# Adding x off TensorE for more output blocks, with query sums and query turns moved, in a fused attention and highway kernel

## The chip, the core and the metric

The kernel runs on one core of a Trainium2 chip. The metric is the device time of one execution in microseconds, as the median of several runs. All times below are in microseconds (us) unless marked ns. PE is TensorE, DVE is VectorE, ACT is ScalarE, POOL is GpSimd, SP is SyncE, which here only issues DMAs.

## The reference

For 8 batches with 8 heads, 576 tokens and a head width of 64, linear attention comes first, then a highway layer over 4608 rows of 512 features:

```python
q_s = softmax(q, axis=-1)          # over the 64 features of a head
k_s = softmax(k, axis=2)           # over the 576 tokens
kv  = einsum('bhsd,bhse->bhde', k_s, v)
x   = einsum('bhsd,bhde->bhse', q_s, kv)   # then heads side by side: 4608 x 512
H   = maximum(x @ w_h, 0)
T   = 1 / (1 + exp(-(x @ w_t + b_t)))
out = T * H + (1 - T) * x
```

Inputs and output are fp32; the kernel computes matmuls in fp16 and leaves out the subtraction of the maxima, which cancels.

## The kernel before, in words

**Tiles.** The unit of the attention part is a batch b, that of the highway part a chunk c of 512 columns, which is the batch of that number. Token s of a batch is 9p + n, so a batch has nine groups n of 64 tokens; n = 0 to 7 make up the chunk, and the ninth tokens (n = 8) of all batches are kept in x9 and done at the end as chunks 8 and 9, with 256 columns each. x is held with features on partitions, in four blocks ob (or k_) of 128 features. Two batches make a pair g = c // 2 (0 to 3), for the output has 128 rows per token group of a pair.

**Attention of a batch b.** exp_half (L183, ACT) takes exp of q and of k, half of the heads at a time. q_sums (L234, DVE, two instructions of 1.35) and q_recip (L252, DVE) give the reciprocal row sums, and q_scale_p (L264, POOL, 1.90 and 2.33) scales the queries. These then must be turned, features to partitions: for b up to 5 by q_trans (L69, PE, in three parts, each copied out by DVE at L282), for b = 6 and 7 by q_turn (L291), two transposing DMAs on SP's queue. cast_v (L195, POOL, two instructions of 1.15) casts v. kv_half (psk, PE) multiplies exp(k) and v, kv_norm (L222 and L223, DVE) divides, and x_pair (px, PE) multiplies by the turned queries, in two halves, each cast into xT by ACT (L354). With left=True it does the ninth tokens too, first of all in the first half, and x9_copy (L315, DVE) stores them.

**Highway, by chunk c and block ob.** W_h has the identity subtracted and is halved, so that

- gate (pt, PE, then tanh on ACT at L383) gives t = tanh((x W_t + b)/2),
- carry (ph on PE, then dd on DVE at L401) gives dd = max(-x/2, (x W_h - x)/2) = (H - x)/2,
- blend (DVE, L409) gives g = (t + 1) dd = T (H - x), in fp16.

The output is g + x. It is turned back to rows by matmuls with the identity (turn_block, L424), 128x128 each: one matmul for g and, accumulated in the same bank, one for x, unless add_x (L416, POOL) has added x to g in SBUF before. Which blocks are added so is listed in `added` (L414): blocks 0 and 1, and for the last pair also 2. out_tile(g, n) turns the four blocks of one token group of a pair and copies the bank to SBUF, mostly on ACT (L458); four of them are stored by one DMA. For the last pair (spare=True) more banks are used and DVE takes part of the copies (L454, L456). tile9 (L470) and last9 (L488) do so for ninth tokens, all with x turned on PE.

**Banks.** gate and carry take their banks from a pool of four (ps_ht). A bank is given out in the order in which banks became free in the program, and the trace shows it: the matmuls of a gate start after the dd of two blocks earlier at the soonest, those of a carry after the blend of two blocks earlier. q_trans and the ninth tokens of x_pair share one bank (q1), psk and x_pair share another two (q2), and out_tile has one of its own (nat).

**Order.** Each engine works through its instructions in program order. From chunk 1 on, that order is a list written by hand: `at(p, ...)` puts a step at position p, and the list is run by rising p, in the order of the calls where p is equal. Chunk c has gate(c, ob) at 8c + 2 ob, carry one later and blend two later, so one unit of p is half a block. Batch b has its steps around p = 8(b - 1) (L541), with offsets by batch (L543 to L563). The change's parts are all offsets in this list, the two lists of added blocks, the engine of some additions, and the copy of last9.

Of the kernel before, what the change touches and what calls it, by code (L numbers as in the profile page):

```python
# [18 lines left out]
def kernel(  # L19
# [10 lines left out]
    nc = tc.nc  # L30
    B, H, S, D = q.shape
    P = 128
    PAD = 128
    N9 = S // 64
# [46 lines left out]
    x9 = consts.tile([P, 4, B, 64], FP16, name="x9")  # L81
    g9 = consts.tile([P, 4, B, 64], FP16, name="g9")
# [77 lines left out]
    def two_banks(name, dt=FP32):  # L160
        return ps_2.tile([P, 2, 2048 // (4 if dt is FP32 else 2)], dt, tag="q2", name=name)
# [202 lines left out]
    def views(c):  # L364
        if c >= B:
            h = slice(4 * (c - B), 4 * (c - B) + 4)
            return lambda k_: x9[:, k_, h], lambda k_: g9[:, k_, h]
        g, b2 = c // 2, c % 2
        if g not in gT:
            gT[g] = gp.tile([P, 4, NM, 2, 64], FP16, tag="g", name=f"g_{g}")  # L370
        return lambda k_: xT[g][:, k_, :, b2, :], lambda k_: gT[g][:, k_, :, b2, :]
# [39 lines left out]
        )  # L411


    added = lambda g: (0, 1) if g < 3 else (0, 1, 2)  # L414

    def add_x(c, ob):  # L416
        xv, gv = views(c)
        nc.gpsimd.tensor_add(gv(ob), gv(ob), xv(ob))  # L418


    o32 = {}
# [2 lines left out]
    def turn_block(t, k_, xs, us):  # L424
        dst = t[:, k_, :]
        if xs is not None:
            mm(dst, xs, ident, True, False)
        mm(dst, us, ident, xs is None, True)

    def flat(t):  # L430
        return t.rearrange("p k d -> p (k d)")
# [35 lines left out]
    def blk9(t, g, k_):  # L467
        return t[:, k_, 2 * g : 2 * g + 2].rearrange("p b d -> p (b d)")

    def tile9(g, nk):  # L470
        if g % 2 == 0:
            o32["9", g // 2] = og.tile([P, 4, 512], FP32, tag="o32", name=f"o9_{g}")
        ps, tag = ((ps_1, "q1"), (ps_nat, "nat"))[g % 2]
        t = ps.tile([P, 4, P], FP32, tag=tag, name=f"nat9_{g}")
        for k_ in range(nk):
            turn_block(t, k_, blk9(x9, g, k_), blk9(g9, g, k_))
        o = o32["9", g // 2][:, g % 2, 0 : nk * P]
        if g % 2:
            nc.vector.tensor_copy(o, flat(t)[:, 0 : nk * P])
        else:  # L480
            nc.scalar.copy(o, flat(t)[:, 0 : nk * P])
        if g % 2:
            nc.sync.dma_start(
                rows9[:, g - 1 : g + 1, 0 : nk * P],
                o32["9", g // 2][:, 0:2, 0 : nk * P],
            )

    def last9():  # L488
        o9 = o32["9", 1]
        t = ps_ht.tile([P, 4, P], FP32, tag="ht", name="nat9_l")  # L490
        for i in range(2):
            turn_block(t, i, blk9(x9, i + 2, 3), blk9(g9, i + 2, 3))
        nc.scalar.copy(o9[:, 0, 384:512], t[:, 0])
        nc.vector.tensor_copy(o9[:, 1, 384:512], t[:, 1])
        nc.sync.dma_start(rows9[:, 2:4, 384:512], o9[:, 0:2, 384:512])


# [2 lines left out]
    def at(p, *fs):  # L500
        events.setdefault(p, []).extend(fs)

    E = lambda f, *a: (lambda: f(*a))

    for c in range(1, B + 2):
        for ob in range(4):
            p = 8 * c + 2 * ob
# [6 lines left out]
    for g in range(B // 2):  # L514
        p = 16 * (g + 1)
        if g < B // 2 - 1:
            for i in range(8):
                at(p + 2 + 2 * i, E(out_tile, g, i))
        else:
            for i in range(8):  # L520
                at(p + 1 + i, E(out_tile, g, i, True))
    p = 8 * B + 8
    at(p + 3, E(tile9, 0, 4))
    at(p + 4, E(tile9, 1, 4))
    at(p + 8, E(tile9, 2, 3), E(tile9, 3, 3), E(last9))

    at(8, E(cast_v_head, 2, 0, nc.gpsimd), E(q_scale_p, 2, 0, 4), E(q_scale_p, 2, 4, 8))
# [3 lines left out]
    at(10, E(cast_v_head, 2, 1, nc.scalar), E(exp_half, 2, "k", 1))  # L531
    at(10.5, E(blend, 0, 3))
    at(12.5, E(add_x, 0, 0), E(add_x, 0, 1), E(add_x, 1, 0))
    at(14.5, E(add_x, 1, 1))
    for c in range(2, B):
        for ob in added(c // 2):
            at(8 * c + 2 * ob + 2.5, E(add_x, c, ob))
    at(11, E(cast_v_head, 2, 2, nc.gpsimd), E(cast_v_head, 2, 3, nc.scalar))
    at(11, E(q_scale_p, 2, 8, N9))
    for b in range(2, B):  # L540
        p = 8 * (b - 1)  # L541
        if b > 2:
            e0, e1, s0, s1, sc = {  # L543
                3: (-2.6, -1.6, -1.1, -0.1, 1),
                4: (-5.5, -4.5, -2.8, -1.5, -1.4),
                5: (-5, -4, -3.4, -2.7, -2.6),
                6: (-6, -5, -4.9, -3.9, -3.8),
                7: (-6, -5, -4.9, -3.9, -3.8),
            }.get(b, (-5, -4, -3.9, -2.9, -2.8))
            at(p + e0, E(exp_half, b, "q", 0))  # L550
            at(p + e1, E(exp_half, b, "q", 1))
            at(p + s0, E(q_sums, b, 0))
            at(p + s1, E(q_sums, b, 1), E(q_recip, b))
            at(p + sc, E(q_scale_p, b, 0, 4), E(q_scale_p, b, 4, N9))
            s = p + {3: 0, 4: 0}.get(b, -0.5)
            at(s, E(exp_half, b, "k", 0), E(cast_v, b, 0))
            at(s + 0.9, E(cast_v, b, 1))
            at(s + 1, E(exp_half, b, "k", 1))
        tr, kv, x = {
            2: ((5, 6, 7.1), (4, 6.2), (6.5, 7.2)),  # L560
            3: ((3.5, 4.9, 4.95), (4, 4), (5.9, 6.9)),
            4: ((2, 3, 4), (4.5, 4.5), (5.9, 6.9)),
        }.get(b, ((2, 3, 4), (4, 4), (5, 6)))  # L563
        if b in turned:
            at(p - 2.05, E(q_turn, b, 0, 4), E(q_turn, b, 4, N9))
        else:
            for i in range(3):
                home = (lambda: two_banks("pq_t", FP16)[:, 0]) if b < 4 and i == 2 else None
                at(p + tr[i], E(q_trans, b, i, home))
        at(p + kv[0], E(kv_half, b, 0))  # L570
        if b == 2:
            at(p + kv[0], E(kv_norm, b, 0, 1))
            at(p + kv[1], E(kv_half, b, 1), E(kv_norm, b, 1, 2))
        else:
            at(p + kv[1], E(kv_half, b, 1), E(kv_norm, b))
        homes = (nat_bank, single) if b == 2 else None
        at(p + x[0], E(x_pair, b, 0, "AA" if b == 2 else "A", b > 2, homes))
        at(p + x[1], E(x_pair, b, 1, "AV" if b == 2 else "A", b > 2, homes))
# [70 lines left out]
```

## Time and profile before

| | us |
|---|---|
| median of 6 runs (131.12 to 132.03) | 131.54 |
| the profiled execution | 132.03 |
| its span, first to last instruction | 130.3 |
| PE busy (1395 matmuls) | 112.7 |
| DVE busy | 97.1 |
| ACT busy | 92.2 |
| POOL busy | 70.3 |

The profile is of one execution: for every instruction its start and length, and for idle time the instruction whose completion ended it. In a line such as `67.14 1.01 ACT L354 CAST ... [0.32 <-PE px L64]` the first number is the start from the beginning of the span, the second the length, and the bracket says how long the engine had been idle and for whom it waited. On DVE and ACT an instruction's record overlaps the next one's by up to 0.1, so distances are best taken from start to start. The mean granted TensorE clock was 0.992 of full speed. The DMA engines were busy nearly all of the time up to 86 us, with the loads of q, k and v, and partly so after that. In the last part, from 113 us, the last pair's output and the ninth tokens' work are interleaved.

### The profile page before, as it was taken

How to read it: one execution, taken by the hardware profiler on the slowest of the kernel's cores; microseconds unless marked ns; L12 is line 12 of the kernel's file. 1: busy time of each engine (PE TensorE's matmuls, PEld its weight loads, DVE VectorE, ACT ScalarE, POOL GpSimd, SP SyncE). 2: the span in 40 equal slices, each digit the busy share in tenths (PEclk: the TensorE clock that was granted, in tenths of full speed). 3: DMA queues.
4: the chain of work that ended last, by engine and by line, in shares of the span. 5: the costliest groups of instructions: out<-in, count | busy, mean ns of one | idle time of the engine just before them, and what ended most of it. 6: DMA issues, size and time to landing. Idle time of an engine off the chain costs nothing.

```text
span 130.3 us, 3405 instructions
## 1 busy us (share of the span) xinstructions
PE 112.7 (87%) x1395; PEld 62.2 (48%) x1395; DVE 97.1 (75%) x179; ACT 92.2 (71%) x130; POOL 70.3 (54%) x64
## 2 busy tenths in 40 slices
PE   4978996886967899999799998997979999999930
PEld 1325442353424445455454654453535455688920
DVE  1387355899799999799789899759945566769950
ACT  3553049994998679679899987996985757565520
POOL 2003436691289999709974983992899504500000
PEclk9999999999999999999999999999999999999996
DMA  3999999999999999999999999999059007065873
GB/s 115 368 379 373 398 401 411 413 410 412 406 410 413 401 410 411 409 407 377 331 400 405 358 273 408 408 241 373 15 115 378 15 0 327 0 282 244 362 296 115
DMA packets 20584, 41.25 MB, mean 317 GB/s; under 512 B 5460, under 2 KB 5976, under 8 KB 19544
## 3 DMA queue, kind: packets, MB, share of 16 engines
q1 hardware_dynamic: 20568, 41.03, 84.7%
q8 instruction: 11, 0.18, 0.5%
q14 instruction: 5, 0.04, 0.1%
HBM read 30.41 MB, written 9.44 MB: 306 GB/s over the span
## 4 chain that ended last, share of the span: by engine, by line
PE 34%; DVE 21%; POOL 14%; DMA 11%; issue 7%; ACT 6%; SPq 3%; DVEq 0%; POOLq 0%; ACTq 0%
PE pt L64 12%; DMA q<-in_q_dram 11%; PE ph L64 11%; POOL eq L264 8%; PE nat L64 5%; DVE dd L401 5%; DVE g L409 4%; DVE r L234 4%; POOL g L418 4%; PE psk L64 2%; ACT eq L183 2%; SPq L96 2%; PE pq L69 2%; PE px L64 2%; POOL v L195 2%
## 5 line engine op out<-in xcount | busy, mean ns | idle before, releaser
L264 POOL TENSOR_TENSOR eq<-eq,r 128x1024 f16<-128x1024 f16 (+2 forms) x16 | 29.7, 1872 | 14.4 <-DVE r L252 13.9
L64 PE MATMUL pt<-xT,w16t 128*128 128x512 f16 x128 | 34.0, 379 | 2.0 <-DVE dd L401 1.2
L64 PE MATMUL ph<-xT,w16h 128*128 128x512 f16 x128 | 33.3, 380 | 1.5 <-ACT w16h L116 1.1
L383 ACT ACTIVATE pt<-pt,bt 128x512 f32<-128x512 f32 (+1 forms) x40 | 24.8, 623 | 11.1 <-PE pt L64 9.8
L401 DVE SCALAR_TENSOR_TENSOR dd<-xT,ph 128x512 f16<-128x512 f16 x32 | 21.7, 679 | 8.1 <-PE ph L64 8.1
L409 DVE SCALAR_TENSOR_TENSOR g<-pt,dd 128x512 f16<-128x512 f32 (+1 forms) x40 | 25.2, 633 | 3.0
L418 POOL TENSOR_TENSOR g<-g,xT 128x512 f16<-128x512 f16 x18 | 20.5, 1151 | 7.4 <-DVE g L409 7.4
L64 PEld LDWEIGHTS <-w16t 128*128 128x128 f16 x160 | 14.7, 98 | 17.8 <-issue 5.1
L183 ACT ACTIVATE eq<-q 128x1152 f16<-128x1152 f32 x16 | 18.2, 1177 | 4.7 <-DMA q<-in_q_dram 4.7
L183 ACT ACTIVATE ek<-k 128x1152 f16<-128x1152 f32 x16 | 18.6, 1175 | 1.8 <-DMA k<-in_k_dram 1.8
L234 DVE TENSOR_REDUCE r<-eq 128x18 f32<-128x1152 f16 x12 | 16.2, 1346 | 4.8 <-ACT eq L183 4.8
L64 PEld LDWEIGHTS <-w16h 128*128 128x128 f16 x160 | 13.6, 98 | 11.7 <-ACT w16h L116 2.9
L195 POOL CAST v<-v 128x1152 f16<-128x1152 f32 x12 | 13.5, 1146 | 10.3 <-DMA v<-in_v_dram 10.3
L64 PE MATMUL nat<-ident,g 128*128 128x128 f16 x142 | 17.8, 219 | 1.2 <-POOL g L418 0.8
L64 PEld LDWEIGHTS <-g 128*128 128x128 f16 x144 | 13.7, 98 | 7.8 <-POOL g L418 1.2
L458 ACT COPY o<-nat 128x512 f32<-128x512 f32 x26 | 15.6, 602 | 0.4 <-PE nat L64 0.3
L354 ACT CAST xT<-px 128x1024 f16<-128x1024 f32 x10 | 10.2, 1016 | 5.3 <-PE px L64 5.3
L64 PE MATMUL warm<-wide,ident 128*128 128x512 f16 x41 | 11.7, 430 | 1.8 <-DVE wide L153 1.8
L69 PE MATMUL pq<-ident,eq 128*128 128x128 f16 x104 | 8.5, 219 | 3.4 <-DVE r L258 1.2
L69 PEld LDWEIGHTS <-eq 128*128 128x128 f16 x108 | 6.8, 98 | 7.6 <-POOL eq L264 2.3
L282 DVE COPY qsT<-pq 128x1024 f16<-128x1024 f16 (+1 forms) x16 | 9.3, 586 | 1.2 <-PE pq L69 0.7
L357 ACT CAST xT<-px 128x512 f16<-128x512 f32 x8 | 4.3, 590 | 7.8 <-PE px L64 7.8
(56 smaller groups left out, 108.8 us busy)
## 6 DMA issues: line engine op xcount, KB each, us to landing
out_dram<-o SPq DMA_DIRECT2D x8, 1024.0 KB, 4.6
q<-in_q_dram SPq DMA_DIRECT2D x7, 1152.0 KB, 13.9
k<-in_k_dram SPq DMA_DIRECT2D x7, 1152.0 KB, 13.2
v<-in_v_dram SPq DMA_DIRECT2D x5, 1152.0 KB, 13.9
v<-in_v_dram SPq DMA_DIRECT2D x6, 576.0 KB, 11.6
q<-in_q_dram SPq DMA_DIRECT2D x2, 576.0 KB, 4.2
k<-in_k_dram SPq DMA_DIRECT2D x2, 576.0 KB, 7.3
w32t<-in_moe_w_t_dram SPq DMA_DIRECT2D x1, 1024.0 KB, 11.6
```

What stands on the lines that cost most here:

```text
L64: mm = lambda o, l, r, st, sp: nc.tensor.matmul(o, l, r, start=st, stop=sp, skip_group_check=True)
L69: nc.tensor.matmul(o, i, ident, is_transpose=True, start=True, stop=True, skip_group_check=True,)
L183: nc.scalar.activation(dst[b][:, :, 2 * a : 2 * a + 2, :], in32[which][b][:, 2 * a : 2 * a + 2].rearrange("p c n d -> p n c d"), AF.Exp,)
L195: (eng or nc.gpsimd).tensor_copy(o, i)
L234: nc.vector.reduce_sum(qsum[b][:, :, h], eq[b][:, :, h, :], axis=AX.X)
L264: nc.gpsimd.tensor_mul(e, e, r.broadcast_to(list(e.shape)))
L354: copy[how](dst, t2.rearrange("p c (n d) -> p c n d", d=64))
L383: nc.scalar.activation(ps, ps, AF.Tanh, bias=bt2[:, ob : ob + 1], scale=0.5)
L401: nc.vector.scalar_tensor_tensor(dd, xv(ob), -0.5, ps, op0=ALU.mult, op1=ALU.max)
L409: nc.vector.scalar_tensor_tensor(gv(ob), th, 1.0, dd, op0=ALU.add, op1=ALU.mult)
L418: nc.gpsimd.tensor_add(gv(ob), gv(ob), xv(ob))
L458: nc.scalar.copy(o, flat(t))
```

## The change

- A third block (2) of pairs 1 and 2, the second and third pair, the fourth block (3) of the last pair, all four blocks of chunk 8 and blocks 0 and 1 of chunk 9 get x added before they are turned; the x matmuls of these blocks are left out of out_tile and tile9.
- For odd chunks the last of these additions (block 2 of chunks 3 and 5, block 3 of chunk 7) is on DVE, the others are on POOL. In chunk 7 and the ninth tokens the additions stand nearer behind their blends.
- The tiles of the last pair stand one position later.
- last9 copies its two blocks with one ACT instruction, not one on ACT and one on DVE.
- Batches 6 and 7: both query sums, formerly around the norm of the batch before (one ahead of it, one behind), stand behind it, and q_scale_p follows later, its second part 0.6 behind its first. The turning DMAs stand one position later.
- Batch 3: the first part of q_trans stands behind the following gate and output tile. Batch 4: its three parts stand about one position later, the third behind kv_half, kv_norm and the first sum of batch 5.

```diff
-    added = lambda g: (0, 1) if g < 3 else (0, 1, 2)
+    added = lambda g: ((0, 1), (0, 1, 2), (0, 1, 2), (0, 1, 2, 3))[g]
+    added9 = lambda g: (0, 1, 2, 3) if g < 2 else (0, 1)
...
-        nc.gpsimd.tensor_add(gv(ob), gv(ob), xv(ob))
+        late = ob == (3 if c == B - 1 else 2) and c % 2 and c < B
+        eng = nc.vector if late else nc.gpsimd
+        eng.tensor_add(gv(ob), gv(ob), xv(ob))
...
-            turn_block(t, k_, blk9(x9, g, k_), blk9(g9, g, k_))
+            turn_block(t, k_, None if k_ in added9(g) else blk9(x9, g, k_), blk9(g9, g, k_))
...
-        nc.scalar.copy(o9[:, 0, 384:512], t[:, 0])
-        nc.vector.tensor_copy(o9[:, 1, 384:512], t[:, 1])
+        nc.scalar.copy(o9[:, 0:2, 384:512], t[:, 0:2])
...
-                at(p + 1 + i, E(out_tile, g, i, True))
+                at(p + 2 + i, E(out_tile, g, i, True))
...
-    for c in range(2, B):
-        for ob in added(c // 2):
-            at(8 * c + 2 * ob + 2.5, E(add_x, c, ob))
+    for c in range(2, B + 2):
+        for ob in added(c // 2) if c < B else added9(2 * (c - B)):
+            at(8 * c + 2 * ob + (2.5 if c < B - 1 else 2.02), E(add_x, c, ob))
...
-                6: (-6, -5, -4.9, -3.9, -3.8),
-                7: (-6, -5, -4.9, -3.9, -3.8),
+                6: (-6, -5, -3.95, -3.1, -3),
+                7: (-6, -5, -3.95, -3.1, -3),
...
-            at(p + sc, E(q_scale_p, b, 0, 4), E(q_scale_p, b, 4, N9))
+            at(p + sc, E(q_scale_p, b, 0, 4))
+            at(p + sc + (0.6 if b > 5 else 0), E(q_scale_p, b, 4, N9))
...
-            3: ((3.5, 4.9, 4.95), (4, 4), (5.9, 6.9)),
-            4: ((2, 3, 4), (4.5, 4.5), (5.9, 6.9)),
+            3: ((4, 4.9, 4.95), (4, 4), (5.9, 6.9)),
+            4: ((3, 4, 4.9), (4.5, 4.5), (5.9, 6.9)),
...
-            at(p - 2.05, E(q_turn, b, 0, 4), E(q_turn, b, 4, N9))
+            at(p - 1.05, E(q_turn, b, 0, 4), E(q_turn, b, 4, N9))
```

## The prediction

> **What bounds the kernel now.** I read the page first (busy shares, slices, groups), then the chain that ended last in order of time, then the timelines of PE, DVE, ACT and POOL from 46 us on, line by line, mapped to the ordered list of steps; then the waits, and the DMA issues of the transposes.
>
> The page gives PE 87% of the span, DVE 75%, ACT 71%, POOL 54%; no share decides alone. Of the groups, shapes kept apart (count | busy us, mean ns | idle before, who ended it), these are touched:
>
> ```profile
> L418 POOL TENSOR_TENSOR g<-g,xT 128x512 f16<-128x512 f16 x18 | 20.5, 1151 | 7.4 <-DVE g L409 7.4
> ...
> L234 DVE TENSOR_REDUCE r<-eq 128x18 f32<-128x1152 f16 x12 | 16.2, 1346 | 4.8 <-ACT eq L183 4.8
> ...
> L64 PE MATMUL nat<-ident,xT 128*128 128x128 f16 x56 | 9.7, 219 | 0.0
> ```
>
> The chain in order of time (start, length, what) shows PE bounding most of 63 to 74, then DVE, PE, ACT, DVE, POOL, and PE alone from 97 to 118:
>
> ```profile
> 58.82 4.20 POOL eq L264 x2
> 63.02 0.05 issue
> 63.06 0.62 PE pq L69 x8
> ...
> 87.40 1.35 DVE r L234
> 88.75 0.60 DVE g L409
> 89.35 0.10 DVE rz L222
> ...
> 93.60 2.33 POOL eq L264
> 95.93 1.12 POOL g L418
> 97.09 0.45 PE nat L64 x5
> ```
>
> PE's timeline, in brackets the idle time just before: the four waits that the moved steps touch are kv norms behind a sum (78.50, 89.95), a v cast (87.83) and an added x (97.09).
>
> ```profile
> 78.50 0.22 PE L64 MATMUL px_l<-qsT,kvn 64*64 64x64 f16 x2 [0.44 <-DVE kvn L223]
> ...
> 87.83 0.48 PE L64 MATMUL psk<-v,ek 64*64 64x65 f16 x36 [0.26 <-POOL v L195]
> ...
> 89.95 0.22 PE L64 MATMUL px_l<-qsD,kvn 64*64 64x64 f16 x2 [0.68 <-DVE kvn L223]
> ...
> 97.09 0.23 PE L64 MATMUL nat<-ident,g 128*128 128x128 f16 x1 [0.82 <-POOL g L418]
> ```
>
> **The change, part by part.** Below, D is the time after minus the time before of the same PE step.
>
> *Removed matmuls.* Eight in each of three pairs (24), eight in the first two ninth tiles and four in the other two (12). Six turn matmuls take 0.34 in the chain, so 0.057 each: 2.05 us of PE in all. It counts only where PE sets the pace.
>
> *Added x.* POOL gets nine adds: three of 128x512 at 1.15 (its own row) and six of 128x256, at 0.61 by the 128x256 row of its scaling. They fall in its idle time, except add_x(4,2), which takes the place of add_x(4,1) between batch 6's scaling and its v casts. DVE gets three adds of 128x512 fp16. No such row exists; 128x288 took 0.31 and 128x1024 0.69, the nearest, 128x576, 0.45: I take 0.42, with 0.31 and 0.69 as ends (work is added, so no gain). The Trainium skill speaks against this: "GPSIMD Engine Reference", section 1 (Specifications), says the two engines share SBUF interfaces and contend when a DVE instruction has two SBUF inputs, which add_x has; two of them run beside POOL's scaling. The trace has one such meeting, DVE's add of 128x288 beside POOL's subtraction, against the same add alone:
>
> ```profile
> 21.35 0.42 DVE L246 TENSOR_TENSOR t<-t 128x288 f16<-128x288 f16 x1
> ...
> 33.93 0.31 DVE L246 TENSOR_TENSOR t<-t 128x288 f16<-128x288 f16 x1
> ```
>
> POOL's subtraction went from 0.43 (20.42) to 0.70 (22.21). Read as blocking, the rule would make add_x(5,2) wait out up to a whole 2.33 scaling; the row says a third more: 0.55. I take 0.55; blocking would cost about 0.7 there, since the scaling running then has that long to go.
>
> *Batch 3's turn, later.* PE idles before its first transposes at 49.94 until POOL's scaling is done. With gate(2,2) and out_tile(0,1) first, the gate starts at 49.59 and kv_half(3) is done at 52.12 instead of about 52.50; then the copy, the norm (kvn 52.79 instead of 53.18) and the second and third transposes follow in turn, and carry(2,2) starts at 52.95 instead of 53.36. Recip(4) and POOL's scaling of 4 (58.82) go with it. D = -0.41.
>
> *Batch 4's turn, later.* The idle time before 63.06 is filled with carry(3,1) and gate(3,2). But kv_half(4,1) waits for POOL's second v cast anyway: it follows the scaling by 2.23 (65.18 before, 64.80 after), so psk is done at 65.33, not earlier than D says. What is new: the copy of the third transposes, before at 65.03, in DVE's idle time ahead of the norm, now stands behind q_sums(5,0), and x_pair(4,0) on PE needs it first of all (ninth token, and the bank). DVE: norm 65.36 to 65.99, sum 65.91 to 67.25 (1.26 apart from the next), copy to 67.45. x_pair(4,0) starts at 67.50 instead of 66.61: a new PE wait of about 1.2, D = +0.89. Queued behind it on PE is everything, on ACT the cast of its output. DVE's dd(3,2) and recip(5) still come 0.2 early.
>
> *add_x(3,2) on DVE.* It pushes DVE by 0.35 to 0.5 (start to start), but with PE late DVE has idle time before dd(4,0) (72.5 to 72.93): nothing. Without that cover it costs its 0.35 at the copy before q_trans(5,1), 74.44. D = +0.8 there, and +0.75 at kv_half(5) after two shorter tiles.
>
> *Late sums, batch 6.* Now the norm of 5 needs only psk: done 77.85, kvn 78.52, and x_pair(5,0) starts right behind carry(4,2) at 78.72: the 0.44 is gone, D = +0.22. Both sums follow (moved past blend(4,1) and the third copy, whose start they no longer hold), so recip(6) starts at 81.07 instead of 79.74: 0.75 of D and 0.58 of DVE idling for psk. On POOL the scaling is moved past add_x(4,1), which runs in idle time before it; the chain after it keeps its length: scaling 81.62 to 85.8 (4.19), add_x(4,2) 1.11, casts 2.25 to 89.1. So kv_half(6,1) starts at 89.15 instead of 87.83: the wait of 0.26 becomes about 1.5 in two pieces, D = +1.32. This is where most of the gain goes.
>
> *Late sums, batch 7.* With the norm ahead of the sums the 0.68 goes: x_pair(6,0) at 90.53, D = +0.58. DVE from the norm: before, norm to the end of blend(4,3) took 5.36 with one sum in it (77.82 to 83.18); with two sums and an add 5.36 + 1.26 + 0.5 = 7.1, so blend(5,3) ends at 96.8. PE banks go back by dd and blend, so gates (6,0) and (6,1) lose about 0.4 and 0.25 to DVE. out_tile(2,0) no longer waits: add_x(5,1) now runs ahead of scaling 7 (-0.82, with its queueing). Carry(6,1) starts at 97.24 instead of 97.38: D = -0.14. Scaling 7 ends at 97.6; the casts end at 99.8, against kv_half(7,1)'s 99.69: D = 0 at x_pair(7,0), 101.2.
>
> *Query turns by DMA, later in the list.* SP's queue has nothing between the old and the new place, so they move past no DMA; they go when their scaling is done. Batch 6's second half goes at 85.85 (before 84.51), batch 7's at 97.65 (95.96). The view of DMA issues has landings of 3.1, 3.4 and 6.0 us. With 3.4, batch 7's lands at 101.05, just ahead of x_pair(7,0); hidden, with 0.15 to spare.
>
> *PE alone, 102 to 113.* ACT sets gate(7,0), so five shorter tiles count: 5 x 0.057 = 0.28. D = -0.28 at carry(8,0).
>
> *The tail.* DVE works from 116.08 almost without a break, but idled 0.90 just before. New: add_x(7,3) (+0.36), on which out_tile(3,0) waits (PE: last block at 114.57); PE is then half a microsecond ahead as tiles have four matmuls, not five or eight; the first copy out of the two banks stays at about 116.1, but dd(8,1) is by then done. With tiles one step later, dd and blend of one block no longer follow each other, which saves the 0.10 to 0.17 between dependent instructions four times (0.5). The POOL adds of the ninth tokens (0.61 after each blend) end at 120.4, as tile9 reaches them. Blend(9,3) ends at 124.1 instead of 125.03. One ACT copy of 128x256 takes the place of ACT 0.27 then DVE 0.29: between the 128x128 row (0.27) and the 128x384 row (0.48), 0.37; but SP needs 0.4 for the DMA before it, so this saves 0.1. The stores of pair 3 follow their copies (the second at 120.7, before 121.1) and are not the last. The last DMA is issued at about 125.1 instead of 126.09.
>
> *The sum.* -0.41 + 1.30 - 0.67 + 1.10 - 0.74 - 0.72 + 0.14 - 0.28 - 0.68 = -0.96 (the D's in order: -0.41, +0.89, +0.22, +1.32, +0.58, -0.14, 0, -0.28, -0.96). Against the profiled execution (span 130.3, 132.03 in all, 0.49 above the median) that is 129.3 and 131.1; against the median 131.54, 130.6.
>
> **The rivals.** *(a) The tail keeps its bound.* DVE is full there and gets an add more; if the 0.90 comes back as a wait for add_x(7,3) and the two-bank copy, only D = -0.28 remains: 131.3. For: DVE's copy waited for ACT's at 116.08, and ACT's place is no earlier. Against: 0.5 of the saving is in DVE's own order.
> *(b) Slower: a late transpose.* Batch 6's first turn took 6.0 to land while loads filled the DMA engines (busy share 1.0 to 85). If the second half, issued 1.34 later, takes 6.0, it lands at 91.85 and x_pair(6,0) starts 1.37 after my 90.53: 132.0. It decides from 4.7 us on. Against: the loads drain by about 87, and the second half before was in use at 89.95, at most 5.4 after its issue.
> *(c) The new wait at x_pair(4,0) is short.* If the copy isn't behind the sum, D stays near 0 there, and all after runs about 0.9 earlier down to the tail: 129.7. Against: the list fixes DVE's order.
>
> **How the numbers follow.** Forecast 130.6 with 0.44; (a) 131.3, 0.24; (b) 132.0, 0.16; (c) 129.7, 0.16. About 0.3% (0.39 us, so 131.15 and 131.93) is what a measurement of this kernel can tell from no change. Faster: nearly all of the forecast, all of (c), a little of (a): 0.62. Same: most of (a), some of the forecast and of (b): 0.22. Slower: the rest of (b): 0.16. The range reaches from (c) to (b), 129.6 to 132.0.
>
> **What would show it.** Right: PE waiting about 1.2 us for the qsT copy at x_pair(4,0); no wait for kvn at the x_pairs of 5 and 6; a wait of about 1.5 for v casts at kv_half(6); none for added x at out_tile(2,0); PE's x turns down from 70 to 34 (32 of pairs, 2 of ninth tokens), beside 2 in the last tile as before. Wrong: POOL's casts of batch 6 not later, transposes awaited by PE, DVE adds of over 0.7, or a tail from carry(8,0) to the last DMA not about 0.7 shorter.

## The result, and the profile after

The kernel after takes 130.86 us (median), the kernel before 131.76 in the runs beside it: ratio 0.993, 95% interval 0.9914 to 0.9947, that is 0.9 us saved. The forecast was 130.6. That it came so close was luck: two errors of nearly 0.9 us, of opposite sign, cancelled.

The profiled execution after took 130.41 us with a span of 128.6. From the page (busy time of engines, and DMA queues):

```profile
PE 111.1 (86%) x1359; PEld 60.9 (47%) x1359; DVE 99.7 (78%) x181; ACT 92.4 (72%) x130; POOL 77.4 (60%) x73
...
q8 instruction: 10, 0.16, 0.5%
```

PE has 36 matmuls fewer. Queue q8 carries instructions, 16 KB a packet; before it had 11 packets. That small difference turns out to matter.

The groups that answer to those shown of before, shapes kept apart (count | busy us, mean ns | idle before):

```profile
L421 POOL TENSOR_TENSOR g<-g,xT 128x512 f16<-128x512 f16 x21 | 23.9, 1154 | 7.9 <-DVE g L409 7.9
...
L234 DVE TENSOR_REDUCE r<-eq 128x18 f32<-128x1152 f16 x12 | 16.0, 1345 | 4.2 <-ACT eq L183 4.2
...
L64 PE MATMUL nat<-ident,xT 128*128 128x128 f16 x32 | 6.1, 219 | 0.0
L421 POOL TENSOR_TENSOR g<-g,x 128x256 f16<-128x256 f16 x6 | 4.0, 667 | 5.4 <-DVE g L409 5.4
L421 DVE TENSOR_TENSOR g<-g,xT 128x512 f16<-128x512 f16 x3 | 3.0, 985 | 0.1
```

The x turns and POOL's adds are as counted (0.67 for 0.61). VectorE's three adds average 0.985 us, where 0.42 to 0.55 was taken; a mean can hide a spread, so here they are one by one (DVE's timeline):

```profile
69.42 1.77 DVE L421 TENSOR_TENSOR g<-g,xT 128x512 f16<-128x512 f16 x1
...
94.59 0.76 DVE L421 TENSOR_TENSOR g<-g,xT 128x512 f16<-128x512 f16 x1
...
114.06 0.42 DVE L421 TENSOR_TENSOR g<-g,xT 128x512 f16<-128x512 f16 x1
```

The same instruction takes 0.42, 0.76 or 1.77. POOL's timeline at the slowest:

```profile
69.01 1.90 POOL L264 TENSOR_TENSOR eq<-eq,r 128x1024 f16<-128x1024 f16 x1 [2.91 <-DVE r L252]
...
70.87 2.51 POOL L264 TENSOR_TENSOR eq<-eq,r 128x1280 f16<-128x1280 f16 x1
```

The add that began at 69.42 ended at 71.19, 0.28 after POOL's scaling (69.01 + 1.90 = 70.91); the one at 94.59 ended 0.28 after the scaling of 93.17, also 1.90 long; the one at 114.06 met no POOL instruction. POOL's next instruction takes 2.51 instead of its usual 2.33. So the add does not run slower beside POOL; it waits until POOL's running instruction is over. The kernels below repeat it: of 26 such adds in twelve traces, the 12 that met no POOL instruction took 0.42 to 0.43, and the 14 that met a scaling all ended 0.28 after it, with POOL's next instruction at 2.51 or 2.52.

PE's timeline at the four kinds of wait shown of before:

```profile
66.62 0.22 PE L64 MATMUL px_l<-qsT,kvn 64*64 64x64 f16 x2 [1.13 <-DVE qsT L282]
...
78.45 0.22 PE L64 MATMUL px_l<-qsT,kvn 64*64 64x64 f16 x2
...
87.80 0.48 PE L64 MATMUL psk<-v,ek 64*64 64x65 f16 x36 [0.70 <-POOL v L195]
...
88.89 0.48 PE L64 MATMUL psk<-v,ek 64*64 64x65 f16 x36 [0.61 <-POOL v L195]
...
90.27 0.22 PE L64 MATMUL px_l<-qsD,kvn 64*64 64x64 f16 x2
...
96.86 0.33 PE L64 MATMUL nat<-ident,g 128*128 128x128 f16 x3
```

The new wait at x_pair(4,0) is there (1.13). The waits for kv norms (78.45, 90.27) and for added x (96.86) are gone: no bracket. The wait for v casts grew to 0.70 + 0.61. And the chain in order of time around the first add:

```profile
66.57 0.60 DVE dd L401
67.17 1.27 DVE r L234
68.46 0.38 DVE r L252
68.84 0.56 DVE g L409
69.42 1.77 DVE g L421
71.19 0.34 DVE x L315
71.53 0.60 DVE dd L401
```

From 64.5 to 74.9 the chain stays on DVE alone, and the add is its longest piece. The prediction had it in idle time.

**Comparing profiles piece by piece.** Single executions differ by 1 us and more in the part ahead of carry(2,1), where the first loads are awaited and nothing was changed (48.71 before, 47.41 after). So I divide each span at PE steps behind that: *body* from the start of carry(2,2) to that of carry(7,3), *end* from there to the issue of the last store (SP's timeline), *landing* from its issue to its landing. In unchanged code these repeat to 0.1 (before, and the kernels tail_only and tail_fewer below, have bodies of 58.41, 58.42, 58.42).

| | body | end | landing | sum | ratio of run times to before (95%) |
|---|---|---|---|---|---|
| before | 58.41 | 14.32 | 3.21 | 75.94 | 1 |
| after | 59.42 | 13.78 | 2.31 | 75.51 | 0.993 (0.9914 to 0.9947) |
| body_only | 59.41 | 14.31 | 3.34 | 77.06 | 1.0018 (0.9985 to 1.005) |
| tail_only | 58.42 | 13.78 | 3.84 | 76.04 | 1.0016 (0.9991 to 1.0042) |
| turn4_back | 59.22 | 13.78 | 2.40 | 75.40 | 0.993 (0.9901 to 0.9959) |
| sums_back | 60.21 | 13.78 | 2.31 | 76.30 | 1.0004 (0.9975 to 1.0034) |
| before_shift | 58.51 | 14.32 | 2.36 | 75.19 | 0.9914 (0.9884 to 0.9944) |
| fetch_back | 59.88 | 13.78 | 3.65 | 77.31 | 1.0091 (1.0059 to 1.0123) |
| tail_shift | 58.42 | 13.78 | 2.95 | 75.15 | 0.9989 (0.9959 to 1.0018) |
| no_add3 | 57.58 | 13.78 | 2.30 | 73.66 | 0.9789 (0.9754 to 0.9825) |
| tail_fewer | 58.42 | 13.78 | 2.38 | 74.58 | 0.9878 (0.983 to 0.9926) |
| add3_clear | 58.84 | 13.77 | 2.41 | 75.02 | 0.9856 (0.9808 to 0.9905) |
| best | 57.65 | 13.77 | 2.40 | 73.82 | 0.98 (0.9737 to 0.9863) |
| best_few | 57.64 | 13.78 | 2.30 | 73.72 | 0.9789 (0.9718 to 0.986) |

Kernels with the later turn of batch 3 gain about 0.37 more ahead of the body (carry(2,1) to carry(2,2), 4.28 where POOL isn't late, 4.65 before). So after saves by this table 0.43 + 0.37 = 0.80 us; the runs say 0.92. Reckoned so, the table agrees with the runs to 0.4 us for all kernels but body_only, add3_clear and tail_shift, which are 0.5 to 0.65 off. Against before, the body of after lost 1.01, its end gained 0.54, its landing gained 0.90.

### The profile page after: what moved, and what is told of

Read it like the earlier page. It is cut to its first block, busy times and chain, and to the rows that moved or that the text cites. A ratio compares the mean times of both kernels' runs of the same rounds, so it can differ in the third digit from the quotient of the medians.

```text
span 128.6 us, 3346 instructions
## 1 busy us (share of the span) xinstructions
PE 111.1 (86%) x1359; PEld 60.9 (47%) x1359; DVE 99.7 (78%) x181; ACT 92.4 (72%) x130; POOL 77.4 (60%) x73
## 4 chain that ended last, share of the span: by engine, by line
DVE 31%; PE 27%; POOL 13%; DMA 8%; SPq 7%; issue 6%; ACT 4%; DVEq 0%; POOLq 0%; ACTq 0%
PE ph L64 8%; DMA w32h<-in_moe_w_h_dram 8%; PE pt L64 8%; POOL eq L264 8%; DVE r L234 8%; DVE dd L401 6%; DVE g L409 5%; SPq L96 4%; POOL v L195 4%; PE nat L64 4%; SPq L111 3%; PE pq L69 3%; PE psk L64 2%; DVE qsT L282 2%; DVE kvn L223 2%
## 5 line engine op out<-in xcount | busy, mean ns | idle before, releaser
L421 POOL TENSOR_TENSOR g<-g,xT 128x512 f16<-128x512 f16 x21 | 23.9, 1154 | 7.9 <-DVE g L409 7.9
L64 PE MATMUL nat<-ident,g 128*128 128x128 f16 x142 | 16.0, 219 | 0.7 <-DVE g L409 0.4
L64 PEld LDWEIGHTS <-g 128*128 128x128 f16 x144 | 12.5, 98 | 7.6 <-DVE g L409 1.1
```

The costliest lines, as they stand in the source:

```text
L64: mm = lambda o, l, r, st, sp: nc.tensor.matmul(o, l, r, start=st, stop=sp, skip_group_check=True)
L421: eng.tensor_add(gv(ob), gv(ob), xv(ob))
```

## The experiments

**Which half gains?** The theory then: the end of the kernel pays, the body about breaks even. In *tail_only* the kernel before gets only the new end:

```diff
-    added = lambda g: ((0, 1), (0, 1, 2), (0, 1, 2), (0, 1, 2, 3))[g]
+    added = lambda g: ((0, 1), (0, 1), (0, 1), (0, 1, 2, 3))[g]
```

The offsets of batches 3, 4, 6 and 7, q_scale_p and q_turn are as before too.

> The kernel before with only the end changed: fourth block of the last pair and ninth tokens added off TensorE, the last pair's tiles one position later, one copy in last9. The theory (gains add up stage by stage: 0.28 by carry(8,0), 0.68 in the tail) expects about 0.7 us less than the kernel before (ratio 0.995), with the profile equal up to carry(8,0) and about 0.7 shorter from there to the last DMA. Rival (a), that DVE keeps the tail's bound, expects no gain (1.000).

Measured: 1.0016. The end is 0.54 shorter, and nothing comes of it: the last store lands in 3.84 us instead of 3.21. *body_only* is the other half, after with the end as before:

```diff
-    added = lambda g: ((0, 1), (0, 1, 2), (0, 1, 2), (0, 1, 2, 3))[g]
-    added9 = lambda g: (0, 1, 2, 3) if g < 2 else (0, 1)
+    added = lambda g: ((0, 1), (0, 1, 2), (0, 1, 2), (0, 1, 2))[g]
+    added9 = lambda g: ()
...
-                at(p + 2 + i, E(out_tile, g, i, True))
+                at(p + 1 + i, E(out_tile, g, i, True))
```

The offset of add_x in chunk 7 and last9's two copies are as before too, and the fourth block is not added.

> The changed kernel with the end as before (the last pair adds three blocks, no ninth tokens added, tiles and last9 as before); third block of pairs 1 and 2, late sums and late turns stay. The theory expects about 0.28 us less than the kernel before (0.998), all of it from shorter tiles after x_pair(7,0). The rival, that the body brings the gain, expects 0.9 less (0.993).

Measured: 1.0018. Neither half gains alone, yet together they save 0.7%. The halves don't add up; something must be shared, and the column of landings shows where: 3.84 and 3.34 in the halves, 2.31 in the whole.

*turn4_back* is after with the turn of batch 4 at its old place:

```diff
-            4: ((3, 4, 4.9), (4.5, 4.5), (5.9, 6.9)),
+            4: ((2, 3, 4), (4.5, 4.5), (5.9, 6.9)),
```

> The changed kernel with batch 4's three turns where they were before (only that offset undone). The theory, that the copy behind q_sums(5,0) is a new wait on the path, expects x_pair(4,0) without its wait of 1.1 and, since all after it follows, up to 0.9 us less than the changed kernel (about 0.986 of the kernel before). The rival, that DVE's added x and POOL's casts for kv_half(6) set the pace after it anyway, expects the time of the changed kernel (0.993).

Measured: 0.993, the same as after, though the wait at x_pair(4,0) is gone. PE's timeline says where the time went:

```profile
71.80 0.38 PE L64 MATMUL pt<-xT,w16t 128*128 128x512 f16 x1 [1.26 <-DVE dd L401]
```

PE waits 1.26 for DVE a few steps later, behind add_x(3,2), which takes 1.77 here too (69.04). In after the two delays lie in parallel: PE is late anyway, so part of DVE's loss is hidden; without the one the other shows.

*sums_back* is after with the sums, scalings and turning DMAs of batches 6 and 7 as before:

```diff
-                6: (-6, -5, -3.95, -3.1, -3),
-                7: (-6, -5, -3.95, -3.1, -3),
+                6: (-6, -5, -4.9, -3.9, -3.8),
+                7: (-6, -5, -4.9, -3.9, -3.8),
...
-            at(p - 1.05, E(q_turn, b, 0, 4), E(q_turn, b, 4, N9))
+            at(p - 2.05, E(q_turn, b, 0, 4), E(q_turn, b, 4, N9))
```

q_scale_p's second part is again right behind its first.

> The changed kernel with the sums, scalings and turning DMAs of batches 6 and 7 where they were before. The theory expects the kv norm waits at x_pair(5,0) and x_pair(6,0) and the wait of out_tile(2,0) for added x to come back, and the casts for kv_half(6) to come earlier: 0.7 to 1.0 us more than the changed kernel (0.999 to 1.001 of the kernel before). The rival, that the late sums only move waits about, expects the time of the changed kernel (0.993).

Measured: 1.0004, its body 0.79 longer than after's. So the late sums save 0.8 to 1.0 us, given the other edits. Of the signs expected, two came: the wait for the norm at x_pair(5,0) (0.43) and that of out_tile(2,0) for added x (0.92). Two did not: x_pair(6,0) doesn't wait, and the casts for kv_half(6) are no earlier. PE waits 0.84 + 0.61 for them, since both POOL additions of chunk 4 (2.26 together) now stand between the scaling and the casts.

**The landing, and the add.** The view of DMA issues from 117 us on (count, KB each, median us to landing), before and then after:

```profile
q8 instruction: 1, 0.02, 0.4%
issues: line engine op xcount, KB each, median us to landing
...
out_dram<-o SPq DMA_DIRECT2D x1, 384.0 KB, 3.4
out_dram<-o SPq DMA_DIRECT2D x1, 128.0 KB, 3.2
```

```profile
issues: line engine op xcount, KB each, median us to landing
...
out_dram<-o SPq DMA_DIRECT2D x1, 384.0 KB, 2.4
out_dram<-o SPq DMA_DIRECT2D x1, 128.0 KB, 2.3
```

Before, an instruction packet of 16 KB starts at 125.0, between the first and the second of the last three stores; after it is missing, and the two stores shown land 0.9 to 1.0 sooner. tail_only and body_only have one too (124.7, 124.4), turn4_back and sums_back none after 113.5. Theory (F in the expectations): the packets feed PE's instructions, and the one that falls in the last stores is needed only when PE has more than a certain number. Counted with weight loads and 12 records of PE's sequencer, PE has 2802 instructions before, 2770 in body_only, 2762 in tail_only and 2730 in after. Three kernels move it by PE instructions alone, 128 columns wide for 512 in the warm-up at the start, so that it lasts about as long. *fetch_back*, after:

```diff
+    def warm_quarter(n):
+        for _ in range(n):
+            mm(warm[:, 0:128], ident, wide[:, 0:128], True, True)
...
-        E(warm_up, 24),
+        E(warm_up, 12), E(warm_quarter, 48),
```

> The changed kernel with 12 of its 24 first warm-up matmuls of 512 columns replaced by 48 of 128 columns: 36 more PE matmuls, as many as the change removes, in the first 10 us where PE waits for data; the added x and all orders stay changed. Theory F (the last us of the gain comes from a 16 KB instruction load that no longer falls among the last stores) expects such a load near 124 again, the last store's landing at 3.2 or more after its issue in place of 2.3, and about 0.9 us more than the changed kernel (1.000 of the kernel before). The rival (the stores land sooner for another reason, or the matmuls' own time brought the gain) expects the time of the changed kernel (0.993).

Measured: 1.0091, against after about 2.1 us slower, where 0.9 was expected. A packet is back at 123.2 and the last store lands in 3.65 (+1.34). A further 0.46 is in the body, all of it behind carry(6,1), where another packet starts at 99.5 and PE then waits 0.39 for the turning DMA of batch 7. The remaining 0.3 isn't accounted for.

*before_shift* is the kernel before with 48 matmuls more, `E(warm_up, 8), E(warm_quarter, 64)`, so that the packet comes earlier than the last stores:

> The kernel before with 16 of the 24 first warm-up matmuls of 512 columns replaced by 64 of 128 columns: 48 matmuls more, nothing else. Theory F expects the instruction load to come some 4 us earlier (near 120 to 122), the last store to land 2.3 after its issue, and about 0.9 us less than the kernel before (0.993), though PE does more. The rival expects no change or a little more time (1.000 to 1.005).

Measured: 0.9914. The packet starts at 117.5, the last store lands in 2.36, body and end are as before. A kernel with 48 matmuls *more* and nothing else gains as much as the whole change. *tail_shift* is tail_only with the same warm-up:

> The kernel before with the changed end (as in tail_only) and 48 more warm-up matmuls as in before_shift. The step of the prediction on the tail (0.55 to 0.7 sooner from carry(7,3) to the last DMA) and theory F together expect 1.4 to 1.6 us less than the kernel before (0.988 to 0.989). The rival, that the tail itself gives nothing, expects the time of before_shift.

Measured: 0.9989, a miss. In the profile the packet starts at 118.9, beside the first store of the last pair, and the last three stores take 4.24, 2.98 and 2.95 us to land, between before (4.64, 3.39, 3.21) and after (3.33, 2.44, 2.31); by the table it should still have gained 0.8. Why the runs show only 0.1 to 0.3 is left open.

*no_add3* is turn4_back without add_x(3,2): x is not added to block 2 of chunk 3, so this part of the output lacks x.

```diff
-            at(8 * c + 2 * ob + (2.5 if c < B - 1 else 2.02), E(add_x, c, ob))
+            if (c, ob) != (3, 2): at(8 * c + 2 * ob + (2.5 if c < B - 1 else 2.02), E(add_x, c, ob))
```

> The changed kernel with batch 4's turns where they were and without one addition: x is not added to block 2 of chunk 3 at all, so that DVE does not meet POOL's scaling of batch 5 there. The theory that DVE's two-input add waits for the end of POOL's running instruction (1.77 us) and that this is the pace after batch 4 expects carry(4,1) about 1.3 earlier than with the addition, and part of it kept: 0.5 to 1.3 us less than the changed kernel (0.983 to 0.989). The rival, that POOL's casts and the sums of batch 6 set the pace anyway, expects the time of the changed kernel (0.993).

Measured: 0.9789, 1.85 us less than turn4_back in the runs and 1.64 in the body. One add, 0.42 long where nothing blocks it, costs four times that in this order of steps, and more than I had expected of the removal.

**Blocking itself, the count, and a better kernel.** *tail_fewer* is tail_only with 16 warm-ups fewer, so 2730 instructions as in after:

```diff
-        E(warm_up, 24),
+        E(warm_up, 14),
```

Likewise 4 for 6, 2 for 4, and 3 for 5 in warm_mid.

> tail_only (the kernel before with the end of after) with 16 warm-up matmuls fewer in the head (14 for 24, 4 for 6, 3 for 5, 2 for 4), so that PE has as many instructions as in the kernel after (1365, counted as matmuls with their weight loads: 2730 records against tail_only's 2762). Nothing else is changed. Theory of the instruction load: the load that fell among the last stores of tail_only (at 124.7) is gone, the last store lands in about 2.4 us instead of 3.8, and the shorter end shows: 0.992 to 0.995 of before, as turn4_back, whose body takes as long. Rival, the end itself saves nothing whatever is loaded: 1.000 to 1.003 as tail_only. If the fewer warm-ups cost clock in the head, the start of carry(2,1) shows it and the landings decide.

Measured: 0.9878, a larger gain than expected, though the interval reaches into the range. The issues from 117 us on, tail_only and then tail_fewer:

```profile
q8 instruction: 1, 0.02, 0.4%
issues: line engine op xcount, KB each, median us to landing
...
out_dram<-o SPq DMA_DIRECT2D x1, 384.0 KB, 4.0
out_dram<-o SPq DMA_DIRECT2D x1, 128.0 KB, 3.8
```

```profile
issues: line engine op xcount, KB each, median us to landing
...
out_dram<-o SPq DMA_DIRECT2D x1, 384.0 KB, 2.4
out_dram<-o SPq DMA_DIRECT2D x1, 128.0 KB, 2.4
```

Body and end are equal to a hundredth (58.42 and 13.78 in both), and the landing alone falls by 1.46. With the packet gone the shorter end shows in the time. This is the cleanest test of the step, for the landing is counted from the issue, and what fewer warm-ups do at the start doesn't enter it.

*add3_clear* is turn4_back with batch 5's second sum behind the add, which then meets no POOL instruction:

```diff
-                5: (-5, -4, -3.4, -2.7, -2.6),
+                5: (-5, -4, -3.4, -1.45, -1.4),
```

> turn4_back with the second query sum of batch 5 (and its reciprocal, so POOL's scaling of batch 5) behind VectorE's add of x for chunk 3, block 2, which then runs while POOL has nothing to do. Theory of blocking (the add ends when POOL's running two-input instruction ends): the add takes 0.42 us instead of 1.77; the scaling of batch 5 starts some 0.6 to 1.0 later, so that of the 1.35 only 0.4 to 0.7 come through: 0.987 to 0.991 of before, against turn4_back's 0.993. Rival, VectorE's add is slow at that place for another reason (its operands, the banks): 1.5 to 1.8 us again, and 0.996 or more of before, because the scaling is later for nothing.

Measured: 0.9856, body 0.38 shorter than turn4_back's; the runs show 1.0 us, more than the pieces do, and more than expected. DVE's and POOL's timelines:

```profile
67.75 0.42 DVE L421 TENSOR_TENSOR g<-g,xT 128x512 f16<-128x512 f16 x1
```

```profile
70.01 4.19 POOL L264 TENSOR_TENSOR eq<-eq,r 128x1024 f16<-128x1024 f16 x2 [3.96 <-ACT ek L183]
```

The same add, with the same operands, takes 0.42, and POOL's two scalings 4.19 together instead of 4.37. Blocking is shown; that it is slow for another reason is refuted. Of the 1.35 won 0.38 comes through, since the scaling starts at 70.01 for 68.63 in turn4_back, and PE waits 0.80 for its end ahead of q_trans(5,1).

*best* is turn4_back with the second pair's list as before, no add in block 2 of chunks 2 and 3; *best_few* is that with 16 warm-ups for 24:

```diff
-    added = lambda g: ((0, 1), (0, 1, 2), (0, 1, 2), (0, 1, 2, 3))[g]
+    added = lambda g: ((0, 1), (0, 1), (0, 1, 2), (0, 1, 2, 3))[g]
```

> turn4_back with the second pair (chunks 2 and 3) as before: blocks 0 and 1 added, block 2 turned on TensorE, so no VectorE add in chunk 3 and eight turn matmuls more (2746 PE records). The output is whole. Theory of blocking: as no_add3 (0.979) with up to 8 x 0.057 = 0.46 us of PE given back: 0.979 to 0.984, if no instruction load falls among the last stores; with it (last stores landing in 3.3 us and more) 0.987 to 0.991. Rival, no_add3 was fast for another reason than the missing add: 0.990 to 0.994 as turn4_back, with short landings.

> best with 16 warm-ups for 24 at the start, so 2730 PE records as in the kernel after. Theory of the instruction load: no load near the end, last store landing in about 2.4 us, 0.979 to 0.983 of before, equal to best if best has no load there either and 0.7% faster if it has. Rival, the count of PE instructions doesn't matter: the same as best in landing and time.

Measured: 0.98 and 0.9789, both intervals clear of after's (0.9914 to 0.9947). best's body is 57.65: the eight turn matmuls put back cost 0.07 against no_add3. Neither has a packet near the last stores (2746 and 2730 instructions), so the step from 2746 to 2762 holds the point at which it appears, and best_few tells nothing more.

## Why the prediction was near, and where its steps failed

All five of its signs of being right appeared, and two of its signs of being wrong: additions on DVE of over 0.7, and a tail that is 0.48 shorter from carry(8,0) to the last DMA, not about 0.7.

- **Batch 3's turn, −0.41.** Right: 4.28 from carry(2,1) to carry(2,2) for 4.65, where POOL isn't late. In after's own profile POOL's v cast had waited 0.34 for its load, and the distance was 4.65.
- **Batch 4's turn, +1.30.** Right in place, engine and size: a wait of 1.13, and 1.31 more from carry(2,2) to carry(3,3) than before (16.67 for 15.36). What the wait is worth was wrong: rival (c) puts its absence at 0.9, and turn4_back, without it, has the time of after, for then the loss by add_x(3,2), the next point, shows in its place.
- **add_x(3,2) on DVE, "nothing".** Wrong; this is the step that failed most. The prediction took 0.55, from a row of 0.42 for 0.31 beside POOL, and set aside the rule of the Trainium skill in "GPSIMD Engine Reference", section 1 (Specifications). Measured was 1.77. It reckoned blocking for add_x(5,2) alone, at about 0.7 (0.76 measured), and not for add_x(3,2), where the scaling had just begun. The row could not tell a third more from blocking. There were two such meetings before, and this is the second:

```profile
22.21 0.70 POOL L125 TENSOR_TENSOR w32h<-w32h,ident 128x128 f32<-128x128 f32 x1 [0.15 <-DMA w32h<-in_moe_w_h_dram]
...
22.65 0.42 DVE L246 TENSOR_TENSOR t<-t 128x288 f16<-128x288 f16 x1
```

In both, POOL's running instruction had only about 0.25 left, and the add ended 0.16 to 0.17 after it. Waiting for its end cost little there, and comparing ends, not only lengths, would have shown it. The Trainium skill, "SBUF — State Buffer", section "Who interferes with whom", states it outright: a VectorE instruction with two SBUF inputs contends with a POOL instruction that reads SBUF, and the loser fully blocks. The runs agree: 1.77 beside a scaling of 1.90, 0.42 without. The cover named, 0.43 of idle time before dd(4,0), could hide a push of 0.35 to 0.5, not the 1.69 from the start of the add to the next start on DVE. Against the forecast the body is 0.35 late at carry(4,1) and 0.6 at carry(4,2).

- **The late sums.** Their three waits went as foreseen, and the casts' new wait was 1.31 in two pieces for "about 1.5"; that it comes from the late sums is not shown, as sums_back has 1.45 of it without them. The balance, −0.14 at carry(6,1), failed by inheritance: the body is 0.8 late there, most of it from carry(4,2); add_x(5,2), blocked to 0.76 for 0.55, is probably part of the rest. Over the whole body +0.13 was forecast (−0.28 from −0.41) and +1.01 measured.
- **Query turns.** Right: PE never waited for a transpose, so rival (b) didn't occur. Rival (c) didn't either, the wait is there.
- **PE alone, −0.28.** Right: against before, taken from carry(2,2) on, after is 1.23 late at x_pair(7,0) and 0.96 at carry(8,0), so −0.27; and the +0.14 forecast from carry(6,1) to x_pair(7,0) came as +0.17.
- **The tail, −0.68.** −0.48 measured from carry(8,0) to the last issue (12.20 for 12.68), or −0.54 from carry(7,3) as in the table, the same in every kernel with the new end. The mechanism holds, and rival (a) with it falls: dd(8,1) now stands ahead of the first copy out of the two banks, and the idle time before that copy is 0.46 for 0.90. Each piece gained a little less than forecast. That copy comes 0.40 later behind carry(8,0), from it to the end of blend(9,3) takes 0.86 less, and the single last copy saves 0.02 of the 0.1 expected.
- **The landing, taken as constant.** That is the second failed step: what lies behind the last issue fell by 0.90, by an instruction packet that is no longer loaded there. Without it the other three terms come to +0.10, no gain, and fetch_back, with the packet put back, is slower than before.

In sum: −0.41 + 0.13 − 0.68 = −0.96 was forecast, and −0.37 + 1.01 − 0.54 − 0.90 = −0.80 is what the profiles give (the two middle terms are +0.96 and −0.48 when carry(8,0) is the border, as in the prediction). The number was saved by the landing, which was not forecast.

What the runs don't settle: why tail_shift gained so little, 0.3 us of fetch_back, and what exactly adds the last 0.1 to 0.2 of the body behind carry(4,2). That the packets are PE's instructions is inferred: only PE's count was altered, and the packet moved, came and went with it; the queue itself names no engine. The traces speak for it too: the tenth packet starts in all fourteen when PE has begun 2477 to 2497 of its instructions, the eleventh, where there is one, at 2746 to 2792, though by the clock the tenth lies anywhere from 102.9 to 113.3. How the packet delays the stores is open as well. The Trainium skill, "Runtime: NRT & Kernel Launch", section "Instruction fetch mechanics", says that each sequencer fetches its instructions in blocks of 16 KiB over a DMA queue of its own, mostly hidden. The packets' size agrees; hidden it isn't when it lands among the last stores.

## What to carry to other kernels

Before work with two SBUF inputs is moved from POOL or PE to VectorE, look up which POOL instruction runs at that place: beside POOL's scalings the add cost the rest of that instruction, not a share more. To read a row of two engines side by side, compare where the two instructions end. When two halves of a change gain nothing alone and something together, compare the pieces that neither half touches, the landing of the last stores first. And test a small gain against a kernel that only shifts the instruction count, before the gain is put down to the edit.

## What was not expected of the hardware

- A VectorE add of two fp16 SBUF operands (128x512, 0.42 alone) begun while POOL runs a two-input instruction ends 0.28 after POOL's, in all 14 cases seen, and POOL's next instruction is 0.18 longer (2.51 for 2.33). One of 128x288 (0.31 alone) ended 0.16 to 0.17 after, in both cases seen.
- An instruction packet of 16 KB among the last stores delays the landing of the last one by 0.9 to 1.5 us (2.3 to 2.4 without; 3.21, 3.34, 3.65, 3.84 with; 2.95 in tail_shift, where it starts earlier). It can be moved away by adding instructions (48 matmuls, −0.86%) or by leaving out few (16 matmuls, tail_only to tail_fewer).
